# An attention and two-MLP kernel on one core: where block means of V are read from, when weights are decoded, and in which order sums are taken

## The chip, the cores and the metric

One Trainium2 chip, one core. The metric is the device time of one execution, in microseconds. A core has five engines with instruction streams of their own: PE (TensorE, matrix products), DVE (VectorE), ACT (ScalarE), POOL (GpSimd) and SP (SyncE, which here only issues DMAs). Each works through its stream in order and waits on semaphores.

## What is computed

Block-sparse attention feeds two MLPs. The reference, cut to what matters:

```
k_sum = k.reshape(B, H, nb, 32, D).max(axis=3)
v_sum = v.reshape(B, H, nb, 32, D).mean(axis=3)
scores_l = scale * q @ k.T           # kept where |i - j| < 16
scores_s = scale * q @ k_sum.T + log(32)
a = softmax(concat(scores_l, scores_s))
x = a @ concat(v, v_sum)             # B, H, S, D = 2, 8, 768, 64
x = x.reshape(1536, 512)
h = x @ w_in;  x = (h - tanh(h)) @ w_out      # 512 -> 2048 -> 512
a = x @ w1;  b = x @ w2                       # 512 -> 1024
out = ((a * b) @ w3) @ w_out2                 # 1024 -> 1024 -> 512
```

All of it is float32. The large products are taken as three products of fp32r parts (high x high, high x low, low x high), with `split_mm` (L185).

## The kernel before

**Weights.** `Weights` (L60) turns each 128x512 weight chunk, which arrives as 64-bit words, into an fp32 tile and then into a high and a low part. One chunk is a unit: `start` loads it and lets ACT make its size (L108); `unit`, or three times `dve`, lets DVE make the three bit operations L111, L113 and L115; `high` is a cast on ACT (L143), `low` a subtraction on POOL (L150). `need` forces all of it for a chunk that a product is about to read. At most four raw chunks are in SBUF (`NRAW`), so a load on SP waits until DVE is through with an older chunk.

**Attention** (L264 to L490). The 8 pairs of (batch, two heads) are n; each has three groups u of four 64-query tiles, so g = 3n + u runs from 0 to 23, and the loop runs on to 27 to drain. In step g the engines are given: scores of g + 1 (L339), transposes of g - 2 (L367), values of g - 3 (L382), softmax of g (L350 on DVE, L353 on ACT, L360 on POOL). A tile sees a window of 96 keys and 24 blocks. `vg` holds, for every tile, the values of its 96 window keys and, in rows 64 to 87, the 24 block means. These means come from a second copy of V in its natural layout, `vn` (`load_v`, L281): `value_blocks` (L312) multiplies each 128-row piece by a matrix `mean` of 1/32 (6 products per n, each recorded as two), `value_copy` (L322) takes the result from PSUM, and `block_rows` (L326) spreads it into `vg` by three small DMAs. `key_blocks` (L291) makes the block maxima of K, whose last step is a POOL copy into `kt` (L308). `parts` (the table `N34`) spreads the product w3 x w_out2, `w34a`, over the steps; from g = 15 two parts run in each. `busy(8)` (L399) multiplies the identity by itself eight times into an unused bank: before the first scores, and after steps 0 and 1.

**First MLP** (L614 to L635). A step n does one 128-wide column of `w_in` for 512 tokens: `hidden(n)` (L513, tile `ph`), then the curve h - tanh(h) of it (`curve`, L521), and `back(n - 2)` (L545, tile `x`), which multiplies the curve's high and low parts `gh`, `gl` by `w_out`. In each step the loop places `wt.start`, `wt.high`, `evacuate`, `curve` (in which `wt.unit` stands between the end of the curve before and the curve itself), and `wt.low`.

**Second MLP** (L742 to L818). For tokens 512 to 1535 the products with w1 and w2 are taken by a seven-product scheme: `group` (L715) makes seven accumulations `p_w` in four PSUM banks, in the order 1, 6, 5, 7, 2, 4, 3, and combines them on DVE (L668) into four tiles. `w_sums` (L689) prepares the summed weights `s_w` of the next group: two additions of 128x512 (`t0`, `t1`), then four of 128x256. `between` (L776) puts an output product, `final` (L646), between products 5 and 7.

Of the kernel before, what the change touches and what calls it, by code (L numbers as in the profile page):

```python
# [7 lines left out]
F32 = mybir.dt.float32  # L8
# [33 lines left out]
LAG = 2  # L42
NDEC = 3
# [12 lines left out]
def fused_kernel(tc, qT, kT, vN, vW, w_in, w_out, w1, w2, w3, wo2, out):  # L56
# [138 lines left out]
    with tc.tile_pool(name="base", bufs=1) as base, \  # L195
# [19 lines left out]
        mean = base.tile([P, P // BLK + BLK], F32, name="mean")  # L215
        nc.gpsimd.memset(mean, 0.0)
        for i in range(P // BLK):
            nc.gpsimd.memset(mean[i * BLK:(i + 1) * BLK, P // BLK + i:P // BLK + i + 1], 1.0 / BLK)
# [45 lines left out]
        with tc.tile_pool(name="p1", bufs=1) as p1, \  # L264
                tc.tile_pool(name="ps1", bufs=1, space=PSUM) as ps1:
            NG = B * NP * NU
            kt, qt, vn, vg, vrow, st, nm, pr, z = ({} for _ in range(9))
# [13 lines left out]
            def load_v(n):  # L281
                vn[n] = p1.tile([P, S // P, P], F32, tag="vn", bufs=2, name=f"vn_{n}")
                nc.sync.dma_start(out=vn[n], in_=vN[n // NP, n % NP])

            def load_vwin(n):
                vg[n] = p1.tile([P, NQ, P], F32, tag="vg", bufs=2, name=f"vg_{n}")
                nc.sync.dma_start(out=vg[n], in_=vW[n // NP, n % NP])
# [24 lines left out]
            def value_blocks(n, out):  # L312

                pvs[n] = out
                nj = S // P // NBR
                for j in range(nj):
                    for c in range(NBR):
                        o = P // BLK * (1 - j)
                        mm(out=out[c * BLK:(c + 1) * BLK, :], lhsT=mean[:, o:o + BLK], rhs=vn[n][:, c * nj + j, :],
                           start=j == 0, stop=j == nj - 1)  # L320
# [84 lines left out]
            busy(8)  # L405
            load_k(0)
            load_q(0)
            load_v(0)
            wt.load(1)
            load_k(1)  # L410
            load_q(1)
            wt.load(2)
            load_vwin(0)
# [5 lines left out]
            for g in range(NG + 4):  # L419
# [4 lines left out]
                if u == 0 and 0 < n < NN:  # L424
                    load_vwin(n)
                if u == (0 if n else 2) and n + 2 < NN:
                    load_k(n + 2)
                if u == (0 if n else 1) and n + 1 < NN:
                    load_v(n + 1)
# [25 lines left out]
                if g < 2:  # L455
                    busy(8)
# [3 lines left out]
                for i in range(TU):  # L460
# [6 lines left out]
                    if i:  # L467
# [5 lines left out]
                wt.start(2 if g in MORE else 1)  # L473
# [47 lines left out]
        def curve(n, ph, prev):  # L521

            if prev is not None:
                mask, t, g = prev
                nc.vector.copy_predicated(out=g, mask=mask[:, :].bitcast(U32), data=t)  # L525
            wt.unit()
# [6 lines left out]
            if prev is not None:  # L533
                gp[n - 1] = tmp("gh", n, LAG + 1, F32R), tmp("gl", n, LAG + 1, F32R)
                nc.scalar.copy(out=gp[n - 1][0], in_=g)  # L535
                low_part(nc.gpsimd, gp[n - 1][1], g, gp[n - 1][0][:, :])
# [332 lines left out]
```

## Time and profile before

| what | value |
|---|---|
| median of 3 runs | 592.7 us (590.75 to 592.89) |
| profiled execution | 592.24 us, its span 590.4 us |
| PE, share of span and instructions | 97%, 3168 |
| DVE | 79%, 885 |
| ACT | 57%, 741 |
| POOL | 47%, 233 |
| DMA | 59.70 MB, mean 101 GB/s |
| mean granted TensorE clock | 0.994 |

The time of an execution is the span from its first to its last instruction plus about 1.8 us around it. Busy shares are means over stages; the attention stage ends near 129 us, the first MLP near 425 us. A matmul's recorded duration includes its way through the array, so products that follow each other overlap: distance from start to start tells the rate.

### The profile page before, as it was taken

The numbers are of one execution on the slowest core, as the hardware profiler recorded it, in microseconds if no ns is written. First come the engines' busy times: TensorE is split into PE (matmuls) and PEld (weight loads), VectorE is DVE, ScalarE is ACT, GpSimd is POOL, SyncE is SP. The second block draws the span as 40 slices with busy tenths as digits, with TensorE's granted clock in tenths as the row PEclk, the third lists the DMA queues.
The fourth block names the chain that finished last, engine by engine and source line by source line (L and its number), as shares of the span: only waits on it lengthen the run. The fifth ranks groups of instructions, "written<-read, shape, count | busy, mean of one in ns | idle before, by whom it ended". The sixth has DMA issues, their size and how long they took to land.

```text
span 590.4 us, 9062 instructions
## 1 busy us (share of the span) xinstructions
PE 571.6 (97%) x3168; PEld 461.4 (78%) x3168; DVE 465.4 (79%) x885; ACT 338.6 (57%) x741; POOL 278.9 (47%) x233
## 2 busy tenths in 40 slices
PE   8989999998999999999999999999999999999997
PEld 6667777776888888888888888888887777888885
DVE  3789988789999995779999978999577576878510
ACT  3689977868788774466767667765233322222110
POOL 3456555555556652224645522557735624526120
PEclk9989999998999999999999999999999999999999
DMA  8899996653333230012223102223000100000021
GB/s 323 297 323 306 333 298 226 188 162 111 104 108 108 73 106 1 0 37 73 95 84 101 43 1 64 80 71 108 1 0 1 72 0 1 1 2 0 1 90 53
DMA packets 19678, 59.70 MB, mean 101 GB/s; under 512 B 2096, under 2 KB 4784, under 8 KB 19632
## 3 DMA queue, kind: packets, MB, share of 16 engines
q1 hardware_dynamic: 19632, 59.12, 30.8%
q8 instruction: 25, 0.41, 0.3%
q14 instruction: 21, 0.17, 0.1%
HBM read 54.79 MB, written 3.15 MB: 98 GB/s over the span
## 4 chain that ended last, share of the span: by engine, by line
PE 76%; DVE 14%; issue 6%; POOL 2%; ACT 1%; DMA 1%; DVEq 0%; POOLq 0%; ACTq 0%
PE x L187 6%; PE x L188 6%; PE x L186 6%; PE ph L187 6%; PE ph L188 6%; PE ph L186 6%; PE p_w L186 3%; PE p_w L187 3%; PE p_w L188 3%; PE o L188 3%; PE o L186 3%; PE o L187 3%; PE s L339 2%; PE busy L403 2%; PE w L188 2%
## 5 line engine op out<-in xcount | busy, mean ns | idle before, releaser
L150 POOL TENSOR_TENSOR wl<-dec,wh 128x512 fp32r<-128x512 f32 x72 | 111.5, 1553 | 48.9 <-ACT wh L143 41.6
L191 POOL TENSOR_TENSOR gl<-g,gh 128x512 fp32r<-128x512 f32 x48 | 65.8, 1371 | 140.5 <-ACT gh L535 75.3
L186 PE MATMUL x<-gh,wh 128*128 128x512 f32 x192 | 75.4, 393 | 1.8 <-ACT gh L535 1.8
L187 PE MATMUL x<-gl,wh 128*128 128x512 f32 x192 | 75.5, 393 | 1.0 <-POOL gl L191 1.0
L188 PE MATMUL x<-gh,wl 128*128 128x512 f32 x192 | 75.4, 393 | 0.0
L186 PE MATMUL ph<-xh,wh 128*128 128x512 f32 x192 | 74.8, 390 | 0.0
L187 PE MATMUL ph<-xl,wh 128*128 128x512 f32 x192 | 74.7, 389 | 0.0
L188 PE MATMUL ph<-xh,wl 128*128 128x512 f32 x192 | 74.7, 389 | 0.0
L115 DVE SCALAR_TENSOR_TENSOR dec<-raw,dec 128x512 uint32<-128x512 uint32 x45 | 62.4, 1387 | 1.5
L530 ACT ACTIVATE u<-ph 128x512 f32<-128x512 f32 x48 | 28.8, 600 | 54.8 <-PE ph L188 54.8
L143 ACT CAST wh<-dec 128x512 fp32r<-128x512 f32 x72 | 44.5, 623 | 13.3 <-DVE dec L115 13.2
L540 DVE TENSOR_TENSOR g<-ph,u 128x512 f32<-128x512 f32 x48 | 32.7, 682 | 19.8 <-ACT th L531 19.8
L525 DVE COPY_PREDICATED g<-mk,th 128x512 f32<-128x512 uint32 x48 | 41.7, 870 | 4.0
L186 PEld LDWEIGHTS x<-gh,wh 128*128 128x128 f32 x192 | 36.5, 190 | 10.3 <-ACT gh L535 2.2
L353 ACT ACTIVATE pr<-pr,nm 128x120 f32<-128x120 f32 x96 | 37.0, 390 | 12.1 <-DVE nm L350 11.8
L187 PEld LDWEIGHTS x<-gl,wh 128*128 128x128 f32 x192 | 36.4, 189 | 9.0 <-POOL gl L191 1.3
L188 PEld LDWEIGHTS x<-gh,wl 128*128 128x128 f32 x192 | 36.4, 190 | 7.5
L187 PEld LDWEIGHTS ph<-xl,wh 128*128 128x128 f32 x192 | 36.1, 188 | 7.5
L186 PEld LDWEIGHTS ph<-xh,wh 128*128 128x128 f32 x192 | 36.0, 188 | 7.5
L188 PEld LDWEIGHTS ph<-xh,wl 128*128 128x128 f32 x192 | 36.1, 188 | 7.4
L542 DVE SCALAR_TENSOR_TENSOR g<-sq,g 128x512 f32<-128x512 f32 x48 | 40.3, 839 | 0.7 <-ACT sq L538 0.6
L191 POOL TENSOR_TENSOR s_w<-s_w,s_w 128x512 fp32r<-128x512 f32 x16 | 20.4, 1292 | 38.9 <-ACT s_w L704 36.0
(153 smaller groups left out, 1423.0 us busy)
## 6 DMA issues: line engine op xcount, KB each, us to landing
raw<-w SPq DMA_DIRECT2D x32, 512.0 KB
raw<-w_in SPq DMA_DIRECT2D x16, 512.0 KB
raw<-w_out SPq DMA_DIRECT2D x16, 512.0 KB
vg<-vW SPq DMA_DIRECT2D x8, 768.0 KB
raw<-wo SPq DMA_DIRECT2D x8, 512.0 KB
kt<-kT SPq DMA_DIRECT2D x7, 544.0 KB
vn<-vN SPq DMA_DIRECT2D x8, 384.0 KB
qt<-qT SPq DMA_DIRECT2D x7, 384.0 KB
```

The costliest lines, as they stand in the source:

```text
L115: lambda tu=tu, su=su, lo=lo: stt(out=tu, in0=lo, scalar=29, in1=su, op0=ALU.logical_shift_right, op1=ALU.bitwise_or)])
L143: nc.scalar.copy(out=h, in_=self.t[n])
L150: nc.gpsimd.tensor_tensor(out=l, in0=self.t[self.n_low], in1=h[:, :].bitcast(F32), op=ALU.subtract)
L186: mm(out=acc, lhsT=lh, rhs=rh, start=start, stop=False)
L187: mm(out=acc, lhsT=lh, rhs=rl, start=False, stop=False)
L188: mm(out=acc, lhsT=ll, rhs=rh, start=False, stop=stop)
L191: eng.tensor_tensor(out=out, in0=x, in1=high.bitcast(F32), op=ALU.subtract)
L353: nc.scalar.activation(out=pr[g][:, i, :], in_=pr[g][:, i, :], func=AF.Exp, scale=-1.0, bias=nm[g][:, i:i + 1], accum_out=z[g][:, i:i + 1])
L525: nc.vector.copy_predicated(out=g, mask=mask[:, :].bitcast(U32), data=t)
L530: nc.scalar.activation(out=u, in_=ph, func=AF.Square)
L540: nc.vector.tensor_tensor(out=gn, in0=ph, in1=u, op=ALU.mult)
L542: nc.vector.scalar_tensor_tensor(out=gn, in0=sq, scalar=GAM, in1=gn, op0=ALU.add, op1=ALU.mult)
```

## The change

Three separate edits.

1. **Block means from the window tiles.** The copy `vN` and `load_v` go. `value_blocks` reads `vg` instead: 12 tiles of 64 keys per n in place of 6 pieces of 128, so 12 products in place of 6. `mean` is built differently: of a tile's 128 rows, 16 to 47 are the tile's first block, 48 to 63 and 88 to 103 its second; POOL builds these columns with memsets, six `affine_select` and one addition. `vg` gets three buffers in place of two; it is loaded in step u = 1 of the n before, not in u = 0 of its own. Each `busy(8)` becomes `busy(4)`.
2. **First steps of the first MLP.** In steps 0 to 3 (`FIRST`) the curve comes ahead of `wt.start` and of the weight units, and the casts of the step before come ahead of the curve. Steps 0 and 1 decode no unit; in steps 2 and 3 one is decoded behind the curve. The attention's last step decodes and starts none.
3. **Sums in two parts.** `w_sums` yields after its two 128x512 additions; the four 128x256 additions and the casts follow only after the next piece of `group`.

```diff
-        mean = base.tile([P, P // BLK + BLK], F32, name="mean")
+        mean = base.tile([P, 6 + BLK], F32, name="mean")
         nc.gpsimd.memset(mean, 0.0)
-        for i in range(P // BLK):
-            nc.gpsimd.memset(mean[i * BLK:(i + 1) * BLK, P // BLK + i:P // BLK + i + 1], 1.0 / BLK)
+        def rows(col, a, b):
+            nc.gpsimd.memset(col, 1.0 / BLK)
+            for base_, step in ((-a, 1), (b - 1, -1)):
+                nc.gpsimd.affine_select(out=col, in_=col, pattern=[[0, 1]], compare_op=ALU.is_ge, fill=0.0,
+                                        base=base_, channel_multiplier=step)
+        rest = base.tile([P, 1], F32, name="mean_rest")
+        rows(mean[:, 6:7], WIN, WIN + BLK)
+        rows(mean[:, 7:8], WIN + BLK, QT)
+        rows(rest, CW, CW + WIN)
+        nc.gpsimd.tensor_tensor(out=mean[:, 7:8], in0=mean[:, 7:8], in1=rest, op=ALU.add)
...
-                nj = S // P // NBR
-                for j in range(nj):
+                nt = NQ // NBR
+                for j in range(nt):
                     for c in range(NBR):
-                        o = P // BLK * (1 - j)
-                        mm(out=out[c * BLK:(c + 1) * BLK, :], lhsT=mean[:, o:o + BLK], rhs=vn[n][:, c * nj + j, :],
-                           start=j == 0, stop=j == nj - 1)
+                        o = 6 - 2 * j
+                        mm(out=out[c * BLK:(c + 1) * BLK, :], lhsT=mean[:, o:o + BLK], rhs=vg[n][:, c * nt + j, :],
+                           start=j == 0, stop=j == nt - 1)
...
-            busy(8)
+            busy(4)
             load_k(0)
             load_q(0)
-            load_v(0)
             wt.load(1)
+            load_vwin(0)
...
-                if u == 0 and 0 < n < NN:
-                    load_vwin(n)
-                if u == (0 if n else 1) and n + 1 < NN:
-                    load_v(n + 1)
+                if u == 1 and n + 1 < NN:
+                    load_vwin(n + 1)
...
-                    if i:
+                    if i and g < NG + 3:
                         wt.dve(1)
...
-                wt.start(2 if g in MORE else 1)
+                if g < NG + 3:
+                    wt.start(2 if g in MORE else 1)
...
             if prev is not None:
                 mask, t, g = prev
                 nc.vector.copy_predicated(out=g, mask=mask[:, :].bitcast(U32), data=t)
-            wt.unit()
+                if n < FIRST:
+                    high()
+            if n >= FIRST:
+                wt.unit()
...
+            if n < FIRST:
+                cur = curve(n, nxt, cur)
             wt.start()
...
-            wt.high()
+            if LAG <= n < FIRST:
+                wt.unit()
+            if n >= LAG:
+                wt.high()
             closing = len(evac)
             evacuate()
-            cur = curve(n, nxt, cur)
+            if n >= FIRST:
+                cur = curve(n, nxt, cur)
...
                 tt(t, h[:, :].bitcast(F32), add, l[:, :].bitcast(F32))
+            yield
             a, b = slice(0, H * P), slice(H * P, DM)
...
-            lhs = w_sums("w2", m)
-            for _ in range(4):
+            sums = w_sums("w2", m)
+            next(sums)
+            next(g)
+            lhs = next(sums)
+            for _ in range(3):
                 next(g, None)
```

`high()` in `curve` is the pair of the cast `gh` and the subtraction `gl`. The w2 group of each m takes its sums for the next w1 group in the same two parts. The changed file's lines are numbered up to 24 higher.

PE at the start of the program, before (`s` are scores, `pvs` the means of n = 0, `busy` the identity products):

```order
L403 MATMUL busy<-ident 128x128 x8
L339 MATMUL s_176<-kt_151,qt_154 64x120 x8
L339 MATMUL s_185<-kt_151,qt_154 64x120 x8
L403 MATMUL busy<-ident 128x128 x8
L339 MATMUL s_226<-kt_151,qt_154 64x120 x8
L319 MATMUL pvs<-vn_157,mean 32x128 x6
L403 MATMUL busy<-ident 128x128 x8
L339 MATMUL s_291<-kt_161,qt_163 64x120 x8
```

and in the change:

```order
L411 MATMUL busy<-ident 128x128 x4
L347 MATMUL s_173<-kt_150,qt_153 64x120 x8
L347 MATMUL s_182<-kt_150,qt_153 64x120 x8
L411 MATMUL busy<-ident 128x128 x4
L347 MATMUL s_215<-kt_150,qt_153 64x120 x8
L327 MATMUL pvs<-vg_158,mean 32x128 x12
L411 MATMUL busy<-ident 128x128 x4
L347 MATMUL s_278<-kt_160,qt_162 64x120 x8
```

The rows stand in the same places; the identity products are halved and the means doubled.

DVE where attention passes into the first MLP, before (`xl` closes attention, `dec` are weight units, `g` and `th` the curve):

```order
L191 TENSOR_TENSOR xl_122<-av_1920,xh_119 128x256
L113 SCALAR_TENSOR_TENSOR dec_1943<-raw_1853,dec_1943 128x512
L115 SCALAR_TENSOR_TENSOR dec_1943<-raw_1853,dec_1943 128x512
L111 TENSOR_SCALAR dec_1958<-dec_1958 128x512
L113 SCALAR_TENSOR_TENSOR dec_1958<-raw_1896,dec_1958 128x512
L115 SCALAR_TENSOR_TENSOR dec_1958<-raw_1896,dec_1958 128x512
L540 TENSOR_TENSOR g_2011<-ph_1984,u_2007 128x512
L541 TENSOR_TENSOR th_2009<-ph_1984,th_2009 128x512
L542 SCALAR_TENSOR_TENSOR g_2011<-sq_2008,g_2011 128x512
L525 COPY_PREDICATED g_2011<-mk_2010,th_2009 128x512
L111 TENSOR_SCALAR dec_1997<-dec_1997 128x512
```

and in the change:

```order
L192 TENSOR_TENSOR xl_129<-av_1935,xh_126 128x256
L552 TENSOR_TENSOR g_2009<-ph_1992,u_2005 128x512
L553 TENSOR_TENSOR th_2007<-ph_1992,th_2007 128x512
L554 SCALAR_TENSOR_TENSOR g_2009<-sq_2006,g_2009 128x512
L536 COPY_PREDICATED g_2009<-mk_2008,th_2007 128x512
L552 TENSOR_TENSOR g_2041<-ph_2019,u_2037 128x512
L553 TENSOR_TENSOR th_2039<-ph_2019,th_2039 128x512
L554 SCALAR_TENSOR_TENSOR g_2041<-sq_2038,g_2041 128x512
L536 COPY_PREDICATED g_2041<-mk_2040,th_2039 128x512
L552 TENSOR_TENSOR g_2073<-ph_2051,u_2069 128x512
L553 TENSOR_TENSOR th_2071<-ph_2051,th_2071 128x512
L554 SCALAR_TENSOR_TENSOR g_2073<-sq_2070,g_2073 128x512
```

No weight unit stands between the curves of steps 0, 1 and 2; three units come that much later.

DVE in the first w1 group, before (`t_w` and `s_w` are the sums, the last row reads the bank of product 5 for the last time):

```order
L668 TENSOR_TENSOR t_w_0_4994<-wh_3787,wl_3788 128x512
L668 TENSOR_TENSOR t_w_0_4995<-wh_4161,wl_4162 128x512
L668 TENSOR_TENSOR s_w_0_4996<-t_w_0_4995 128x256
L668 TENSOR_TENSOR s_w_0_4996<-s_w_0_4996,t_w_0_4994 128x256
L668 TENSOR_TENSOR s_w_0_4997<-t_w_0_4994,t_w_0_4995 128x256
L668 TENSOR_TENSOR s_w_0_4997<-t_w_0_4994,s_w_0_4996 128x256
L661 COPY u_out_0_5013<-o_0_4577 128x512
L661 COPY gh_out_2_5025<-o_2_4585 128x512
L668 TENSOR_TENSOR a_1_4967<-a_1_4967,p_w_0_5034 128x512
L668 TENSOR_TENSOR ab_0_4968<-a_1_4967,p_w_0_4986 128x512
```

and in the change:

```order
L686 TENSOR_TENSOR t_w_0_5009<-wh_3802,wl_3803 128x512
L686 TENSOR_TENSOR t_w_0_5010<-wh_4176,wl_4177 128x512
L679 COPY u_out_0_5018<-o_0_4592 128x512
L679 COPY gh_out_2_5030<-o_2_4600 128x512
L686 TENSOR_TENSOR a_1_4982<-a_1_4982,p_w_0_5039 128x512
L686 TENSOR_TENSOR ab_0_4983<-a_1_4982,p_w_0_5001 128x512
L686 TENSOR_TENSOR s_w_0_5011<-t_w_0_5010 128x256
L686 TENSOR_TENSOR s_w_0_5011<-s_w_0_5011,t_w_0_5009 128x256
L686 TENSOR_TENSOR s_w_0_5012<-t_w_0_5009,t_w_0_5010 128x256
L686 TENSOR_TENSOR s_w_0_5012<-t_w_0_5009,s_w_0_5011 128x256
```

The four 128x256 sums stand behind the last row that reads the bank; the same happens in the six other groups that prepare sums.

## Rows read from the trace of the kernel before

**Rows 1.** The page's 40 slices, 14.8 us each: busy tenths of PE and DVE.

```profile
PE   8989999998999999999999999999999999999997
...
DVE  3789988789999995779999978999577576878510
```

**Rows 2.** Waits of PE, whole run: waiting line, releaser; total us, times, longest.

```profile
PE s L339 <- POOL kt L308: 4.9, 6, 1.5
PE p_w L186 <- DVE ab L668: 3.2, 3, 1.4
```

**Rows 3.** Timeline of the first 25 us: start, us, engine, line, operation, tiles; idle before.

```profile
1.36 6.77 PE L403 MATMUL busy<-ident 128*128 128x128 f32 x16 [1.36 <-POOL ident masks.py:199]
...
2.19 0.26 POOL L210 TENSOR_SCALAR_AFFINE_SELECT band<-band 64x96 f32<-64x96 f32 x1
...
3.04 0.47 POOL L218 MEMSET mean<- 32x1 f32 x4
...
5.31 0.42 POOL L308 COPY kt<-kb 128x288 f32<-128x288 f32 x1 [0.22 <-DVE kb L307]
...
8.05 3.24 PE L339 MATMUL s<-kt,qt 64*64 64x120 f32 x32
10.09 0.28 DVE L350 CUSTOM_DVE_ANT_0 pr<-s,mask 128x120 f32<-128x120 f32 x1 [4.84 <-PE s L339]
...
11.23 4.32 PE L403 MATMUL busy<-ident 128*128 128x128 f32 x16
...
16.44 0.64 PE L319 MATMUL pvs<-vn,mean 128*32 128x128 f32 x12
...
16.56 0.28 DVE L350 CUSTOM_DVE_ANT_0 pr<-s,mask 128x120 f32<-128x120 f32 x1 [0.47 <-PE s L339]
...
23.02 0.28 DVE L350 CUSTOM_DVE_ANT_0 pr<-s,mask 128x120 f32<-128x120 f32 x1 [3.50 <-PE t L367]
```

**Rows 4.** Windows of 10 us: busy us of each engine, clock, DMA share, GB/s.

```profile
50.00:60.00 10.00, 9.17 (x127) 7.25 (x122) 9.49 (x41) 9.13 (x31) 5.78 (x6) 1.00 0.99 337
```

**Rows 5.** Timeline of PE late in attention, block means of n = 5.

```profile
75.48 0.64 PE L319 MATMUL av<-vn,mean 128*32 128x128 f32 x12
```

**Rows 6.** Timeline of attention's end and the first steps of the first MLP.

```profile
125.50 0.69 DVE L115 SCALAR_TENSOR_TENSOR dec<-raw,dec 128x512 uint32<-128x512 uint32 x1
...
131.62 0.39 PE L186 MATMUL ph<-xh,wh 128*128 128x512 f32 x1
...
133.45 0.59 ACT L530 ACTIVATE u<-ph 128x512 f32<-128x512 f32 x1
133.62 1.48 POOL L150 TENSOR_TENSOR wl<-dec,wh 128x512 fp32r<-128x512 f32 x1 [1.28 <-ACT wh L143]
...
133.99 1.67 DVE L115 SCALAR_TENSOR_TENSOR dec<-raw,dec 128x512 uint32<-128x512 uint32 x1
...
135.03 0.72 ACT L539 ACTIVATE mk<-u,numax 128x512 f32<-128x512 f32 x1
...
137.56 0.73 DVE L525 COPY_PREDICATED g<-mk,th 128x512 f32<-128x512 uint32 x1
...
138.99 0.49 PE L186 MATMUL x<-gh,wh 128*128 128x512 f32 x1 [1.77 <-ACT gh L535]
...
140.50 0.69 PE L187 MATMUL x<-gl,wh 128*128 128x512 f32 x1 [1.02 <-POOL gl L191]
```

**Rows 7.** Windows of 2 us at the first back products; columns as in rows 4.

```profile
142.00:144.00 2.00, 2.00 (x7) 1.52 (x6) 1.86 (x5) 0.96 (x3) 0.14 (x1) 0.50 0.70 242
144.00:146.00 2.00, 2.00 (x10) 1.67 (x9) 1.97 (x2) 2.00 (x4) 1.62 (x2) 0.99 0.05 20
```

**Rows 8.** Timeline of DVE in groups w1 and w2.

```profile
466.44 0.42 DVE L668 TENSOR_TENSOR s_w<-t_w 128x256 f32<-128x256 f32 x1
...
469.89 0.69 DVE L668 TENSOR_TENSOR ab<-a,p_w 128x512 f32<-128x512 f32 x1
...
505.41 0.69 DVE L668 TENSOR_TENSOR b<-b,p_w 128x512 f32<-128x512 f32 x1 [0.53 <-PE p_w L188]
```

More of the change, by code (lines that the diff above doesn't have):

```diff
@@ L42 @@
 LAG = 2
+FIRST = 4
 NDEC = 3
@@ L53, with fused_kernel @@
 SS, SB, GAM = 0.23012508654699032, 0.2896718893925817, 0.2494235093653836
-def fused_kernel(tc, qT, kT, vN, vW, w_in, w_out, w1, w2, w3, wo2, out):
+def fused_kernel(tc, qT, kT, vW, w_in, w_out, w1, w2, w3, wo2, out):
     nc = tc.nc
@@ L266, in fused_kernel @@
             NG = B * NP * NU
-            kt, qt, vn, vg, vrow, st, nm, pr, z = ({} for _ in range(9))
+            kt, qt, vg, vrow, st, nm, pr, z = ({} for _ in range(8))
             def load_k(n):
@@ L279, in load_q @@
                     nc.sync.dma_start(out=qt[n][:, i[0]:i[1]], in_=qT[n // NP, n % NP, :, i[0]:i[1]])
-            def load_v(n):
-                vn[n] = p1.tile([P, S // P, P], F32, tag="vn", bufs=2, name=f"vn_{n}")
-                nc.sync.dma_start(out=vn[n], in_=vN[n // NP, n % NP])
             def load_vwin(n):
-                vg[n] = p1.tile([P, NQ, P], F32, tag="vg", bufs=2, name=f"vg_{n}")
+                vg[n] = p1.tile([P, NQ, P], F32, tag="vg", bufs=3, name=f"vg_{n}")
                 nc.sync.dma_start(out=vg[n], in_=vW[n // NP, n % NP])
@@ L412, in fused_kernel @@
             wt.load(2)
-            load_vwin(0)
             for i in range(3):
@@ L455, in fused_kernel @@
                 if g < 2:
-                    busy(8)
+                    busy(4)
                 wt.high()
@@ L521, in curve, with high @@
         def curve(n, ph, prev):
+            def high():
+                gp[n - 1] = tmp("gh", n, LAG + 1, F32R), tmp("gl", n, LAG + 1, F32R)
+                nc.scalar.copy(out=gp[n - 1][0], in_=g)
+                low_part(nc.gpsimd, gp[n - 1][1], g, gp[n - 1][0][:, :])
             if prev is not None:
@@ L532, in curve @@
                 cur = mask, t, gn
[L533 to L536, printed above, removed]
+            if prev is not None and n >= FIRST:
+                high()
             if ph is not None:
@@ L706, in w_sums @@
                 lhs[i[0]], lhs[i[1]] = (h, l, 0), (h, l, H * P)
-            return lhs
+            yield lhs
         def seventh(acc, lhs, i):
@@ L749, in fused_kernel @@
                 wt.free += [(rawp, "raw", "raw", NRAW)] * NRAW
-                lhs = w_sums("w1", 0)
+                _, lhs = w_sums("w1", 0)
             a = product_a(m, 0)
@@ L800, in fused_kernel @@
             next(g)
-            if m + 2 < NM:
-                lhs = w_sums("w1", m + 2)
+            more = m + 2 < NM
+            if more:
+                sums = w_sums("w1", m + 2)
+                next(sums)
             for a, b in ((a22, b22), (a11, b11), (a21, b21)):
                 next(g)
+                if more and a is a22:
+                    lhs = next(sums)
                 tt(a, a, ALU.mult, b)
@@ L846 @@
     vw[:, :, np.r_[0:QT, CW:NC]] = vp[:, rows].reshape(B, WK, NQ, NP, P).transpose(0, 3, 1, 2, 4)
-    vn = vp[:, WIN:WIN + S].reshape(B, S // P, P, NP, P).transpose(0, 3, 2, 1, 4)
     w3 = moe2_w3.T.reshape(NM // 2, 2, P, NM // 2, 2 * P).transpose(3, 0, 2, 1, 4)
@@ L851 @@
         "kT": kt,
-        "vN": np.ascontiguousarray(vn),
         "vW": vw,
```

## The prediction

> **What bounds the kernel now.** I read the page's slices first, then the waits of PE, then the timeline wherever PE waits. PE is busy in nine tenths of nearly every slice [rows 1], so time is won only where PE stands idle or works slowly. The longest waits are on the block maxima copied by POOL, 4.9 us in six, and on DVE in the second MLP, 3.2 us in three [rows 2]; the start of the first MLP has two more, 1.77 and 1.02 us [rows 6]. In attention the busy share misleads: in the ten microseconds from 50 on, DVE is busy 9.49 and ACT 9.13 of 10 [rows 4], and PE's waits there are the shadow of theirs. So from the first softmaxes until about 75 us DVE sets the pace, and an earlier start of DVE is kept. From 75 us on two weight parts run per step and PE sets it.
>
> All sums start from the profiled execution, 592.24 us, which is 0.46 below the median of the three runs.
>
> **Start of attention.** The first scores wait behind sixteen recorded identity products, 6.77 us from 1.36, although their last input, POOL's copy into `kt`, ends at 5.31 + 0.42 = 5.73 [rows 3]. Halved, the block ends at 4.8 and the copy decides. But POOL has more to do ahead of it: four memsets (0.47 us) become three, with six selects and an addition. If a select costs what a memset does (0.12) that is 0.7 us more, if what the 64x96 select does, started every 0.32 us, 2.1; I take 1.4, near the middle, since the selects wait for each other but are narrow. POOL was free 0.2 us before the copy, so the scores start near 7.0, not 8.05: 1.05 us won.
>
> DVE then has the work from 10.09 to 16.56 less its wait of 0.47, 6.0 us [rows 3], and starts its third softmax near 15.0 (before 16.56). The third one ends 2.96 us later (16.56 to 23.02 less 3.50), at 18.0. The next one waits for the transpose that frees its buffer, which stands on PE behind two more identity blocks of 4.32 us, each halved to 2.16, and behind the means, whose twelve recorded products, about 0.6 us from 16.44, become twenty-four. PE: scores until 10.3, block 12.45, scores 13.4, means 14.6, block 16.75, scores and transpose 1.65 as before (23.02 less the end of the block there, 16.44 + 0.6 + 4.32), 18.4. DVE resumes at about 18.2, not at 23.02: **-4.8**. ACT and POOL had waited with it. Their next loads are covered: SP issues the window tile (768 KB) in the slot after the first weight chunk, 2.2 MB into the queue, done near 8 us at the 337 GB/s of rows 4, and is needed at 13.4. The bounds: POOL's cheaper end gives -5.9; the other end comes from the clock.
>
> An identity pair takes 6.77 / 8 = 0.85 us in the first block and 4.32 / 8 = 0.54 in the second [rows 3]: the array ran at its lower level of 1.2 GHz through all of the first block and reached 2.4 GHz only about when the 32 dense score products ended. So by these rows the identity products do not raise the clock, and fewer of them cost nothing. If without them the clock stayed low until the fourth scores, the blocks would be 3.4 each, the means 2.3, scores and transpose 1.4 more: DVE resumes near 23.3, **+0.3**.
> The Trainium skill (TensorE: Matmul & The Clock Gate, Part 1, "What's actually happening") speaks against the cut: the slow clock is the default and activity is what releases it. By that rule the term would be the +0.3, by the row it is -4.8.
>
> **Means of the later pairs.** Six more products for each of n = 1 to 7, about 0.6 us more on PE each. For n = 1 to 4 DVE sets the pace and PE's wait for the `kt` copy, on average 0.8 us once per pair [rows 2], takes it in. For n = 5, 6, 7 (75.48 [rows 5] and two more like it) PE sets the pace: 3 x 0.6 = 1.8, of which the short waits left there hide a little. **+1.5**; between +0.4 (hidden by the waits) and +2.8 (n = 4 and another exposed as well). What hides the first ones are waits that vanish if DVE gets faster. The removed loads, 8 x 384 KB of 59.7 MB, relieve a queue that is 0.99 busy [rows 4], but no engine waits for a weight chunk there, so I give them nothing of their own.
>
> **Start of the first MLP.** PE ends the third `ph` at 138.99 - 1.77 = 137.2, then waits for `gh` and `gl` of step 0 until 140.50, and its clock falls to the lower level: granted 0.50 in 142 to 144, where 7 products start against 10 in the next two microseconds [rows 6, 7]. Start to start is 0.43 us in place of 0.23 for eight of twelve products, 1.7 us. So 1.77 + 1.02 + 1.7 = 4.5 lost. Step 0's curve is late since ACT's `u` stands at 133.45 behind the cast of a unit, and DVE's part behind the last operation of the next (133.99, 1.67 us), although PE was done with the first `ph` when the second began, at 131.62 [rows 6]. In the change nothing stands between: `u` at 131.8; until `mk` 2.3 us as from 133.45 to 135.75; the predicated copy 0.73; the cast 0.62; POOL's part 1.5 as from the first to the second `x` product: 137.0, and PE needs it at 137.4. No wait remains.
> What pays: three units come three steps later. They are needed from step 12 on, one is decoded per step, and DVE has room near 221 to 266 us (5, 7, 7 tenths [rows 1]). In steps 2 and 3, however, the unit now stands ahead of the predicated copy, so `gl` of steps 2 and 3 comes later. Worked through the order with units of 1.8 us (three operations of up to 0.69), the second of them is 0.3 us late for PE. **-4.2**, between -1.5 (rival 2) and -4.5, all of it.
> That 1.8 rests on POOL being idle then: L115 takes 0.69 us at 125.50 with no POOL instruction beside it, and 1.67 at 133.99, inside POOL's subtraction of 133.62 to 135.10 [rows 6]. With POOL beside both units they end 2 us later, and `gl` of step 3 misses PE by 1.8 in place of 0.3.
> The Trainium skill (SBUF — State Buffer, "Who interferes with whom") has a rule for such pairs: a DVE instruction with two SBUF inputs and a POOL instruction that reads SBUF block each other for the whole instruction. The trace agrees with that, 1.67 against 0.69. By that rule, should POOL run beside them, the term is that of the second rival below, -1.5.
>
> **Groups.** The four half-width sums take 1.65 us of DVE (four of 0.42 from 466.44, 0.41 apart) and stand ahead of the additions that free the bank of product 5, ending with 469.89 [rows 8]. PE waits there in three groups, 3.2 us in all and 1.4 at most [rows 2]; with a restart each, which I put at 0.1, 3.5. Moved behind, the additions end 1.65 earlier, which ends all three waits. But the sums now stand ahead of the addition that frees the bank of the next group's second product, and of the casts and POOL subtractions that feed it; working through, 0.3 comes back after the second, 0.3 after the third, and 0.2 in the later groups, where DVE had waited 0.53 for product 7 [rows 8] and now has the sums behind it. **-2.7**, between -1.0 and -3.5.
>
> **Sum.** -4.8 + 1.5 - 4.2 - 2.7 = -10.2: 592.24 - 10.2 = **582.0 us**. All best ends together give 578.7, all worst 592.8.
>
> **Rivals.**
> 1. *The early start is given back.* The clock stays low, or the loads (0.99 busy in rows 4) cannot be moved forward by 5 us. For: a queue without room; against: a tenth of attention's bytes is gone, and SP waits for free buffers, not for bytes. First term +0.3 in place of -4.8: 587.
> 2. *The wait moves on.* POOL runs beside the units of steps 2 and 3; PE then waits 1.8 us in two pieces at the fourth `x`, and the clock may fall as at 142 [rows 7], another 1.7. The term is -1.5: 585. For: POOL's subtractions follow every step; against: between them it is idle here.
> 3. *Slower: the window tile arrives late.* The means now need 768 KB, issued two steps ahead, about 8.6 us (28 steps in the 121 us from 8 to 129), where 384 KB had been issued three ahead. If issue to landing takes over 8.6 us in a queue 0.99 busy, PE waits in order and everything behind it. At 12 us that is 3.4 us for each of seven pairs, +24 against gains of 10: 606; it turns to a loss from about 10 us per transfer. Against: 768 KB take 2.3 us at 337 GB/s, and about a weight chunk or two stand ahead.
> 4. *Nothing comes of it in attention or the groups*, since DVE's work is the same and only its order differs; half of the transition alone: 590.
>
> **Chances.** Forecast 0.56, rival 1 0.17, rival 2 0.13, rival 4 0.08, rival 3 0.06. A change under 0.5%, 3 us, cannot be told from none here. Forecast and rivals 1 and 2, and a little of 4, lie beyond that: faster 0.87; the rest of 4 is the same, 0.08; rival 3 is slower, 0.05 as it may only eat the gains. The range: from 578, just under the best ends, to 588, which takes in rivals 1 and 2 and leaves out 3 and 4.
>
> **What would show it.** Right: DVE's fourth softmax at 18 to 19 us, first scores near 7; the means' rows twice as many at 0.57 us per twelve; no wait on `gh` or `gl` at the first `x` and clock 1.00 there; no wait of `p_w` on `ab` above 0.4. Wrong: identity pairs at 0.85 beyond 12 us; PE waiting for DMA at the means; a wait on `gl` two steps later; `p_w` waiting for POOL's `s_w`.

## The result, and the profile after

The change takes **584.72 us** (median of four, 583.37 to 587.65) where the kernel before takes 592.73: a ratio of 0.987 with a 95% interval of 0.984 to 0.990, so 8.0 us or 1.3% faster. The forecast was 582.0, the range 578 to 588. The profiled execution of the change took 583.37 us (span 581.7), the fastest of its four; that of before had 592.24 (590.4). So the two traces show 8.7 us, somewhat more than the medians.

Three points of the program split the spans without a gap: the first `ph` product (attention ends on PE), the start of the seventh back product `x`, from which on the steps are 5.44 us apart in both, and the end.

| stretch | before | after | difference | forecast |
|---|---|---|---|---|
| start to first `ph` | 128.77 | 125.63 | -3.1 | -4.8 + 1.5 = -3.3 |
| first `ph` to seventh `x` | 45.87 | 43.67 | -2.2 | -4.2 |
| seventh `x` to the end | 415.76 | 412.4 | -3.4 | -2.7 |

Busy tenths of PE and DVE in the page's 40 slices after, which answer to [rows 1]: the first two slices of PE fall by one each, and DVE is fuller in the first three.

```profile
PE   7889999999999999999999999999999999999997
...
DVE  4999897766999999679999978999668587778610
```

The waits of PE in the whole run of the change (waiting line, releaser; total us, times, longest), which answer to [rows 2]:

```profile
PE s L347 <- POOL kt L316: 5.7, 7, 2.2
PE av L390 <- DMA vg<-vr: 3.1, 3, 1.6
PE x L188 <- POOL gl L192: 1.6, 2, 1.3
PE busy L411 <- POOL ident masks.py:199: 1.4, 1, 1.4
PE w L189 <- POOL wl L151: 0.2, 1, 0.2
```

The wait of `p_w` on `ab` is gone whole. A new one has come: the value products `av` wait for `vg<-vr`, the three small DMAs that spread the block means. Of the 5.7 on `kt`, 2.2 are the start, now that the identity products end before the copy.

The window from 50 to 60 us and the means of the sixth pair after, which answer to [rows 4] and [rows 5]: DVE is as busy as before, the DMA share 0.90 for 0.99, and twice the products take 1.07 us for 0.64.

```profile
50.00:60.00 10.00, 8.66 (x124) 7.00 (x123) 9.49 (x43) 9.57 (x34) 5.67 (x7) 1.00 0.90 288
```

```profile
71.08 1.07 PE L327 MATMUL av<-vg,mean 128*32 128x128 f32 x24
```

The start of the program, timeline after, which answers to [rows 3]:

```profile
1.43 3.36 PE L411 MATMUL busy<-ident 128*128 128x128 f32 x8 [1.43 <-POOL ident masks.py:199]
...
3.29 0.44 POOL L223 TENSOR_SCALAR_AFFINE_SELECT mean<-mean 128x1 f32<-128x1 f32 x2
...
6.48 0.42 POOL L316 COPY kt<-kb 128x288 f32<-128x288 f32 x1
...
6.96 3.47 PE L347 MATMUL s<-kt,qt 64*64 64x120 f32 x32 [2.17 <-POOL kt L316]
...
10.35 2.17 PE L411 MATMUL busy<-ident 128*128 128x128 f32 x8
...
13.42 1.07 PE L327 MATMUL pvs<-vg,mean 128*32 128x128 f32 x24
...
18.25 0.28 DVE L358 CUSTOM_DVE_ANT_0 pr<-s,mask 128x120 f32<-128x120 f32 x1 [0.36 <-PE t L375]
...
21.30 0.69 PE L390 MATMUL av<-pt,vg 120*64 120x64 f32 x16 [1.64 <-DMA vg<-vr]
```

Scores at 6.96 and DVE's fourth softmax at 18.25, 4.77 earlier than before: the forecast said 7.0 and 18.2. POOL's selects take 0.22 us each, and its copy starts 1.17 later than before, as worked (1.4 of new work, less the 0.2 that POOL had been idle). Then the last row takes 1.64 us back.

Attention's end and the first steps of the first MLP, timeline after, which answers to [rows 6]:

```profile
128.68 0.60 ACT L544 ACTIVATE u<-ph 128x512 f32<-128x512 f32 x1 [1.26 <-PE ph L189]
...
131.79 0.75 DVE L536 COPY_PREDICATED g<-mk,th 128x512 f32<-128x512 uint32 x1
...
132.58 0.62 ACT L531 CAST gh<-g 128x512 fp32r<-128x512 f32 x1 [1.03 <-DVE g L536]
...
133.92 0.39 PE L187 MATMUL x<-gh,wh 128*128 128x512 f32 x1
...
134.62 0.50 PE L188 MATMUL x<-gl,wh 128*128 128x512 f32 x1 [0.31 <-POOL gl L192]
...
147.79 0.69 DVE L116 SCALAR_TENSOR_TENSOR dec<-raw,dec 128x512 uint32<-128x512 uint32 x1
...
148.40 0.75 DVE L536 COPY_PREDICATED g<-mk,th 128x512 f32<-128x512 uint32 x1
148.51 0.62 ACT L144 CAST wh<-dec 128x512 fp32r<-128x512 f32 x1 [2.04 <-DVE dec L116]
...
149.05 0.68 ACT L109 ACTIVATE dec<-raw 128x512 f32<-128x512 f32 x1
...
149.49 1.67 DVE L114 SCALAR_TENSOR_TENSOR dec<-raw,dec 128x512 uint32<-128x512 uint32 x1
...
149.63 0.58 ACT L544 ACTIVATE u<-ph 128x512 f32<-128x512 f32 x1
...
150.10 0.58 ACT L545 ACTIVATE th<-ph 128x512 f32<-128x512 f32 x1
...
150.58 0.61 ACT L531 CAST gh<-g 128x512 fp32r<-128x512 f32 x1
...
151.33 1.69 POOL L192 TENSOR_TENSOR gl<-g,gh 128x512 fp32r<-128x512 f32 x1 [0.72 <-PE ph L189]
...
153.07 0.50 PE L188 MATMUL x<-gl,wh 128*128 128x512 f32 x1 [1.32 <-POOL gl L192]
```

The first back product waits 0.31 us in all, where it had waited 1.77 and 1.02. The fourth one, which had waited for nothing, now waits 1.32 for its `gl`. The clock no longer falls, neither at the first back product nor at the fourth; windows of 2 us after, columns as in [rows 7]:

```profile
134.00:136.00 2.00, 1.69 (x8) 1.16 (x7) 1.78 (x3) 1.96 (x4) 0.57 (x1) 1.00 0.00 0
136.00:138.00 2.00, 2.00 (x11) 1.65 (x10) 0.86 (x2) 1.00 (x2) 0.30 (x1) 1.00 0.00 0
...
154.00:156.00 2.00, 2.00 (x11) 1.64 (x10) 1.93 (x4) 1.42 (x3) 0.66 (x1) 1.00 0.43 176
```

DVE in the first w1 group, timeline after, which answers to [rows 8]: the addition that frees the bank stands ahead of the sums, and behind the sums DVE waits 1.68 us for PE.

```profile
463.02 0.69 DVE L686 TENSOR_TENSOR ab<-a,p_w 128x512 f32<-128x512 f32 x1
463.62 0.42 DVE L686 TENSOR_TENSOR s_w<-t_w 128x256 f32<-128x256 f32 x1
...
468.65 0.69 DVE L686 TENSOR_TENSOR b<-u_b,p_w 128x512 f32<-128x512 f32 x1 [1.68 <-PE p_w L189]
```

### The profile page after: what moved, and what is told of

Same layout as the page of the kernel before. It is cut to its first block, busy times and chain, and to the rows that moved or that the text cites. A ratio compares the mean times of both kernels' runs of the same rounds, so it can differ in the third digit from the quotient of the medians.

```text
span 581.7 us, 9203 instructions
## 1 busy us (share of the span) xinstructions
PE 565.4 (97%) x3240; PEld 458.3 (79%) x3240; DVE 462.1 (79%) x885; ACT 339.1 (58%) x741; POOL 280.8 (48%) x239
## 4 chain that ended last, share of the span: by engine, by line
PE 73%; DVE 12%; issue 5%; ACT 3%; DMA 3%; POOL 2%; SPq 0%; POOLq 0%; DVEq 0%; ACTq 0%
PE x L188 6%; PE x L187 6%; PE x L189 6%; PE ph L187 6%; PE ph L188 6%; PE ph L189 6%; PE p_w L187 4%; PE p_w L189 4%; PE p_w L188 4%; PE o L187 3%; PE o L189 3%; PE o L188 3%; PE w L189 2%; PE w L188 2%; PE w L187 2%
## 5 line engine op out<-in xcount | busy, mean ns | idle before, releaser
L116 DVE SCALAR_TENSOR_TENSOR dec<-raw,dec 128x512 uint32<-128x512 uint32 x45 | 60.7, 1348 | 1.5
L192 POOL TENSOR_TENSOR s_w<-s_w,s_w 128x512 fp32r<-128x512 f32 x16 | 22.9, 1449 | 43.5 <-ACT s_w L723 23.5
L536 DVE COPY_PREDICATED g<-mk,th 128x512 f32<-128x512 uint32 x48 | 39.7, 826 | 4.2 <-DVE g L554 0.5
```

Source lines behind the costliest of these rows:

```text
L116: lambda tu=tu, su=su, lo=lo: stt(out=tu, in0=lo, scalar=29, in1=su, op0=ALU.logical_shift_right, op1=ALU.bitwise_or)])
L192: eng.tensor_tensor(out=out, in0=x, in1=high.bitcast(F32), op=ALU.subtract)
```

## The experiments

Twelve kernels in three sets of four, each set timed beside the kernel before; the ratio is to that one. The table splits each profiled execution as above; a profile is one execution, the median stands for all. The column to the first `ph` scatters most: four profiles whose attention code is the change's (the change, no unit in step 3, early cast, unit moved) lie between 125.4 and 129.6, three with that of before (before, first steps alone, sums alone) between 128.8 and 131.2. A difference of two or three microseconds in this column alone shows nothing.

| kernel | median us | ratio to before, interval | to first `ph` | to seventh `x` | to the end |
|---|---|---|---|---|---|
| before | 592.3 to 592.9 | | 128.77 | 45.87 | 415.8 |
| the change | 584.72 | 0.987, 0.984 to 0.990 | 125.63 | 43.67 | 412.4 |
| means alone | 594.26 | 1.003, 1.002 to 1.005 | 129.55 | 47.05 | 416.2 |
| four identity products alone | 589.82 | 0.996, 0.994 to 0.997 | 126.76 | 45.91 | 415.7 |
| first steps alone | 590.02 | 0.997, 0.994 to 1.000 | 131.17 | 43.67 | 415.7 |
| sums alone | 588.9 | 0.995, 0.993 to 0.996 | 128.98 | 45.88 | 412.1 |
| change, no identity products | 583.47 | 0.983, 0.979 to 0.987 | 126.55 | 43.66 | 412.2 |
| change, rows ahead of loads | 588.84 | 0.992, 0.989 to 0.995 | 131.33 | 43.65 | 412.3 |
| change, no unit in step 3 | 591.36 | 0.997, 0.994 to 1.001 | 125.42 | 49.10 | 412.3 |
| change, early cast in step 4 | 585.61 | 0.987, 0.983 to 0.992 | 129.57 | 44.14 | 412.3 |
| change, copy of V loaded again | 589.08 | 0.993, 0.991 to 0.996 | 132.14 | 43.66 | 412.3 |
| four identity products, one copy of V | 588.01 | 0.992, 0.990 to 0.995 | 123.22 | 45.79 | 415.8 |
| change, unit moved to step 4 | 584.77 | 0.987, 0.985 to 0.990 | 127.46 | 43.43 | 412.8 |
| the same, no identity products | 583.63 | 0.985, 0.984 to 0.987 | 125.66 | 43.38 | 412.9 |

**Means alone.** The kernel before with edit 1, `busy(8)` kept:

```diff
-            busy(4)
+            busy(8)
```

(shown against the change; edits 2 and 3 are undone as well).

> The kernel before with edit 1 alone, the identity products left at eight. Theory (the extra products cost PE time in the late pairs, nothing else changes): scores still start near 8.05 us, DVE's fourth softmax moves from 23.0 to about 23.5 because 12 more mean products stand ahead of it, and n = 5 to 7 add 3 x 0.45 = 1.35: 592.2 + 1.9 = 594.1 us. Rival (the waits of the value products for the spread mean rows, 2.7 us in the changed kernel, come from the larger and earlier window transfers and not from the early start): the same waits show here, about 596.8 us.

Measured 594.26, as the theory had it, but not where. In the profile attention is only 0.8 us longer; another 1.2 stand in the transition, where the clock stayed low longer (0.66 over 140 to 150 us, 0.83 before). One wait for the rows is there, 1.1 us. So in this profile's attention the extra products do not show their whole 1.9 us. Its clock has 1.00 from 30 to 35 us, where the profile of before has 0.66: the absent fall pays for part of them, by chance or through the missing copy of V.

**Four identity products alone.** `busy(8)` becomes `busy(4)` in the kernel before.

> The kernel before with the identity products halved and nothing else. Theory (the identity products only delay, and what the start wins is partly given back by the mean rows that arrive through a full queue): scores near 5.9 us, identity pairs at 0.85 us in the first block and 0.54 in the second, DVE's fourth softmax at 17.4 (won 5.6), then 1.5 to 2.7 us of waits for the mean rows: the kernel gains 3 to 4.5, 588 to 589 us. Rival 1 (the queue has room): no such waits, 586.5. Rival 2 (the identity products are what raises the clock): pairs of 0.85 beyond 12 us and no gain, 592.

Measured 589.82, 2.5 us won of the 5.8 that the start alone gives (the fourth softmax at 17.26 for 23.02). PE waits 3.2 us for the rows, and the clock falls. PE's timeline, then windows of 2 us as in [rows 4]:

```profile
21.27 1.12 PE L382 MATMUL av<-pt,vg 120*64 120x64 f32 x16 [1.33 <-DMA vg<-vr]
```

```profile
18.00:20.00 2.00, 0.62 (x4) 0.41 (x4) 1.35 (x5) 1.97 (x6) 0.24 (x1) 0.97 0.81 136
20.00:22.00 2.00, 0.73 (x14) 0.73 (x16) 2.00 (x7) 1.20 (x7) 1.99 (x2) 0.50 0.83 260
22.00:24.00 2.00, 2.00 (x28) 1.46 (x26) 0.83 (x7) 0.93 (x2) 0.00 (x0) 0.50 0.89 278
```

The scores start 1.4 us earlier than in the change, yet the value products start at 21.27, in the change at 21.30. PE is busy 1.35 of the 4 us from 18 to 22 and drops to 1.2 GHz. SP can issue the rows only at 15.76 here: they write into the window tile, whose load has to land first, and SP waits 3.0 us for it (releaser; total us, times, longest):

```profile
SPq L329 <- DMA vg<-vW: 3.0, 1, 3.0
```

The two halves of edit 1, measured alone, give 1.9 - 2.5 = -0.6 us; in the change edit 1 gains more, 2.3 by the medians (8.0 less the 2.3 and 3.4 of the next two runs), 3.1 in the profile.

**First steps alone.** Edit 2 in the kernel before.

> The kernel before with edit 2 alone. Theory (the first two waits and the fall of the clock, 4.5 us, go, and a new wait of 1.3 us for the low part at the fourth back product and some tenths elsewhere stay, whatever attention did before): -2.2, 590.0 us. Rival (the wait at the fourth back product came from the earlier end of attention, not from the order of the first steps): no such wait here and -4.2, 588.0 us.

Measured 590.02, with an interval that just reaches no change; the trace decides. The second stretch is 43.67, to the hundredth that of the change, with the same wait of 1.3 at the fourth back product, which thus belongs to the order of the first steps. (Attention was 2.4 us longer in this execution than in before's, with the same code up to its last step: the clock fell twice in it.)

**Sums alone.** Edit 3 in the kernel before.

> The kernel before with edit 3 alone. Theory (the three waits of the group products on the bank of product 5 go and nothing comes in their place): -3.4, 588.8 us, no wait of a group product above 0.2. Rival (some of it comes back through the later summed weights, as predicted): -2.7 with waits of 0.2 to 0.3 in several groups, 589.5 us.

Measured 588.9; the last stretch is 412.1 for 415.8, and no wait of `p_w` is in the list. Nothing comes back.

**No identity products at all.**

```diff
-            busy(4)
             load_k(0)
...
-                if g < 2:
-                    busy(4)
```

> The changed kernel without any identity product (they feed no output). Theory (the dense score products raise the clock by themselves, and the mean rows, which land near 21.3 us whatever PE does, are a wall): the scores start at 6.96 and take 3.5 us as in the change, the third scores then start one every 0.06 us at 2.4 GHz; DVE's fourth softmax starts near 17, but the first value products still start at 21.3; PE stands idle some 2 us longer before them, the clock falls there as it did at 20 us in the run with four identity products alone, and the time is 585 to 587 us. Rival 1 (without identity products the clock stays at 1.2 GHz beyond the first scores): third scores at 0.1 us each and DVE's fourth softmax at 19 or later, 587 to 589. Rival 2 (no wall): value products near 19, 582.5 to 583.5 us.

Measured 583.47, 1.2 below the change, with overlapping intervals: less than the theory feared. PE in the first 16 us:

```profile
6.88 4.12 PE L347 MATMUL s<-kt,qt 64*64 64x120 f32 x48 [6.88 <-POOL kt L316]
11.24 1.08 PE L327 MATMUL pvs<-vg,mean 128*32 128x128 f32 x24 [0.24 <-DMA vg<-vW]
15.45 1.04 PE L347 MATMUL s<-kt,qt 64*64 64x120 f32 x16 [3.13 <-POOL kt L316]
```

In the change 32 such products take 3.4 us, so the last sixteen take well under a microsecond here, where sixteen take 1.87 at 1.2 GHz (below): the scores alone brought the clock to 2.4 GHz at about 10 us. It fell after the idle 3.13 (0.66 over 15 to 20 us), and the value products started at 22.15, yet attention ended only 0.9 us later than in the profile of the change.

**Rows ahead of the loads.**

```diff
                     block_rows(0)
+                    load_k(2)
+                    load_q(2)
```

(both taken out of their earlier places).

> The changed kernel with the loads of the third pair's keys and queries (928 KB) issued behind the first pair's mean rows instead of ahead of them. Theory (the rows wait in the queue for the bytes issued before them): 928 KB at the 400 GB/s of that stretch are 2.3 us, so the rows land near 19 us instead of 21.3, the wait of 1.64 us at the first value products goes, and attention ends 0.5 to 1.6 us earlier: 583.0 to 584.2 us. Rival (what they wait for is their own small packets, or loads issued after them): the wait stays above 1 us, 584.7.

A miss: 588.84, 4 us slower than the change. The rows did come earlier, at 20.55 for 21.30, and their wait fell from 1.64 to 0.61. But SP now issues the moved loads at 17.56 and 18.29, between the rows and the next weight chunk, and this chunk, issued at 19.04 for 17.23, is late in their place. ACT waits 4.7 us for it, where it waits 1.4 in the change, and PE behind ACT:

```profile
ACT bits L109 <- DMA raw<-wo: 4.7, 1, 4.7
```

```profile
PE t L375 <- ACT pt L380: 2.6, 1, 2.6
```

To reorder the loads in that stretch only changed who waited, here at a loss.

**No unit in step 3 of the first MLP.**

```diff
-            if LAG <= n < FIRST:
+            if n == LAG:
                 wt.unit()
```

> The changed kernel without the weight unit in step 3 of the first MLP; all later units come one step later. Theory (that unit, 1.9 us of DVE, is what makes the curve of step 3 late, and with it the fourth back product): its predicated copy starts near 146.7 instead of 148.4, no wait for the low part at the fourth back product, -1.3 to -1.7, 583.2 us. Rival (the unit that is missing is then needed before it is ready near step 12): the wait goes but PE waits for a weight part later, 584.7 or more.

The rival, and worse: 591.36. The waits of PE:

```profile
PE x L189 <- POOL wl L151: 5.1, 1, 5.1
PE x L188 <- POOL gl L192: 0.3, 1, 0.3
```

The `gl` wait at the fourth back product goes, but the product that waits now, 5.1 us for its weight's low part, is that same fourth one: the unit of step 3 is the chunk that it multiplies by.

**Early cast in step 4.**

```diff
-                if n < FIRST:
+                if n <= FIRST:
                     high()
...
-            if prev is not None and n >= FIRST:
+            if prev is not None and n > FIRST:
                 high()
```

> The changed kernel with the cast and the subtraction of step 3's curve placed ahead of the two ACT operations of step 4, as in the steps before. Theory (the late part is ACT's order at step 4: two operations of 0.58 us stand between the predicated copy's end and the cast): the cast starts near 149.7 instead of 150.58, POOL's subtraction near 150.6 behind its weight part, and the wait of 1.32 us falls to 0.4 to 0.7: -0.6 to -0.9, 584.0 us. Rival (it is DVE's unit in step 3 alone): the wait stays above 1 us.

The wait falls to 0.90, less than expected, and a new one of 0.86 on ACT's copy of a finished `x` appears at the next back product; the stretch is 0.5 longer. No gain in the median. The profile shows something else, in attention, whose code is that of the change:

```profile
10.28 3.35 PE L411 MATMUL busy<-ident 128*128 128x128 f32 x8
13.56 1.87 PE L347 MATMUL s<-kt,qt 64*64 64x120 f32 x16
15.36 1.93 PE L327 MATMUL pvs<-vg,mean 128*32 128x128 f32 x24
17.22 2.74 PE L411 MATMUL busy<-ident 128*128 128x128 f32 x8
```

```profile
21.66 0.28 DVE L358 CUSTOM_DVE_ANT_0 pr<-s,mask 128x120 f32<-128x120 f32 x1 [3.22 <-PE t L375]
```

Identity pairs are 0.84 us apart and the means 0.08 until past 18 us: the array stayed at 1.2 GHz through the dense scores and beyond, although the granted clock is recorded as 1.00 from the start, and the fourth softmax started at 21.66 in place of 18.25.

**The removed copy of V loaded again,** into a buffer that nothing reads, and its counterpart, **four identity products with one copy of V**:

```diff
+                    load_v(n + 1)
```

```diff
-rhs=vn[n][:, c * nj + j, :]
+rhs=vn[0][:, c * nj + j, :]
...
-                if u == (0 if n else 1) and n + 1 < NN:
-                    load_v(n + 1)
```

> The changed kernel with the removed copy of V loaded again (384 KB per pair, which no instruction reads); everything else stays. Theory (until about 60 us attention is short of bytes, so the removed 3.1 MB are what lets the early start last): the mean rows land later than 21.3 us, the waits of PE and ACT for transfers grow and the clock falls again in attention; attention ends 1.5 to 3 us later, 586.2 to 587.7 us. Rival (no engine waits for these bytes, as the prediction has it): 584.7 us, waits as in the change.

> The kernel before with four identity products and the natural copy of V loaded for the first pair only: the block means of the other seven pairs are taken from the first pair's V, so their values are left out. Products as in the kernel before, bytes as in the changed one. Theory (bytes decide): against the run with four identity products alone (589.8) the mean rows land earlier, the clock falls less and 2 to 3 us are won: 587 to 588 us, about the changed kernel's attention less its extra products. Rival (it is the twelve extra products per pair, which shorten PE's idle times, that keep the clock up in the changed kernel): 589 to 590, with the clock falling at 20 us as without them.

Both point to the bytes. Loads that nobody reads cost the change 4.4 us (589.08), and the intervals of the two ratios do not meet; the same bytes left out of the kernel with four identity products win 1.8 (588.01 for 589.82, with intervals that just overlap), without one product more. In the first, the rows of the second pair need 9.4 us from the issue of the first of them to the product that they release, in the change 7.4, and PE waits 3.13 us. In the second, the window tile lands sooner, SP waits 1.4 us for it instead of 3.0 and issues the rows at 13.72 instead of 15.76, and the value products start at 19.39 in place of 21.27, with no fall of the clock up to 130 us:

```profile
37.44 1.13 PE L394 MATMUL av<-pt,vg 120*64 120x64 f32 x16 [3.13 <-DMA vg<-vr]
```

```profile
19.39 0.69 PE L382 MATMUL av<-pt,vg 120*64 120x64 f32 x16 [1.13 <-DMA vg<-vr]
```

```profile
SPq L329 <- DMA vg<-vW: 1.4, 1, 1.4
```

The 4.4 us are not the price of the bytes alone, though. The copy was loaded into one buffer, where the kernel before has two, so SP stood still until the first copy had landed, and with it the loads behind:

```profile
SPq L299 <- DMA vn<-vN: 4.1, 1, 4.1
```

How much of the 4.4 this order took is not shown. The profile of this run had its clock at the lower level until about 16 us.

**The unit of step 3 moved into step 4,** behind the predicated copy and the cast; and the same without identity products:

```diff
             if n >= FIRST:
                 wt.unit()
+            if n == FIRST:
+                wt.high()
+                wt.low()
```

(with the edits of the early cast and of the kernel without the unit in step 3).

> The changed kernel with the unit of step 3 decoded in step 4, behind the predicated copy and the cast of step 3's curve, and cast and subtracted at once. Theory (that unit is the weight chunk of the fourth back product itself; it may stand behind the curve of step 3, whose low part then comes near 149.4 us, and its own low part near 151.4): no wait above 0.4 us at the fourth back product, -1.0 to -1.3, 583.5 us. Rival (DVE, POOL and ACT are full there and the wait only changes its name, as it did when the unit was left out or the cast was moved): a wait of 1 us or more for the weight's low part or for the next steps' curves, 584.7 or more.

> The same, and without any identity product. Theory (the two act in different stages and add): 1.2 us below the run with the moved unit alone, 582.2 us. Rival (the waits for the mean rows decide the end of attention, and without identity products PE only idles longer): no difference to the run with the moved unit alone.

584.77 and 583.63. The 1.32 at the fourth back product becomes 0.62 for the weight's low part, and 0.4 for ACT's copy and longer steps behind make up the rest. The second is 1.1 us below the first, as the change without identity products (583.47) is 1.2 below the change; in both pairs the intervals overlap. So no version was found that is measurably faster than the change without identity products, and that one is ahead of the change by less than the intervals tell apart.

## Why the prediction was right, and where it was not

**The sign, the range and two of three stretches** came out as worked: 584.72 lies within 578 to 588. The profile of the change is 1.4 us above 582.0: +2.0 from the transition, -0.7 from the groups, +0.2 from attention. The median lies another 1.3 above that profile, the fastest of the four executions. The two longest of the four, 587.65 and 585.6, have a mean granted clock of 0.997, the other two, near 583.5, have 0.999. What can lie behind 0.997 is seen in the profile with the unit moved (585.37, 0.997, the same attention code): PE waits 2.1 us for the rows of the second pair, the clock has 0.66 from 35 to 40 us, and attention ends 1.8 later than in the profile of the change.

**Start of attention, -4.8:** to the tenth as far as it was worked (18.25). That it is kept did not hold as put. The sentence "no engine waits for a weight chunk there, so I give them nothing of their own" is the step that failed, along with "their next loads are covered", which looked at the window tile and not at the three small row transfers behind it. They are issued from 14.84 us on and let PE go at 21.30; nor was the first sentence true any more, for ACT waits 1.4 us for a weight chunk there. Against that, the fall of the clock that the kernel before has at 31 to 35 us (0.83 over 30 to 40 us) is absent (1.00). Lead of the change at the mean products of the eight pairs: 3.0, 3.1, 3.8, 5.0, 5.0, 4.4, 4.0, 3.6, then 3.1 at the first `ph`. So the 4.8 was down to 3.1 at the second pair, came back to 5.0 at the fourth, and was spent on means from the fifth on. The forecast of -3.3 for attention was met because two things that it left out cancel in this profile: the wait for the rows and the absent fall of the clock. That it was met to 0.2 is luck, as the scatter of this column shows. That the early start lasts is put down to the bytes by the two runs with them put back and left out; how much of it they pay is open. Rival 1 was right that the queue is full and wrong that everything is given back.

The Trainium skill (DMA: Bandwidth & Descriptors, "Queues, rings and completion order") says that each DMA engine takes the descriptors of a queue in ring order. The trace agrees: with the third pair's loads issued ahead, the rows need 6.5 us from the first issue to the products (14.84 to 21.30), with these behind 5.4 (15.20 to 20.55).

**The clock at the start.** The reading that the clock does not rise in the identity products, and rises in the dense scores, held in the two kernels without identity products (2.4 GHz at about 10 and 12 us). It does not hold every time: in two of the six profiles with the change's start (the early cast, and the copy loaded again) the low level lasted to almost 19 and to 16 us. In the four profiles with eight identity products that was not seen, but four are too few to rule it out. That is the prediction's other end (+0.3), as a matter of chance from one execution to the next; the early cast's profile paid 3.4 us for it. The recorded clock of that profile is 1.000, so the low level at the start does not show in it; the two longer executions of the change, at 0.997, must have had a fall that does, and whether their clock rose late as well no profile shows.
The Trainium skill (TensorE: Matmul & The Clock Gate, Part 1, "What's actually happening") says that the number of slow products at the start of one kernel varies between runs. The profiles agree: the rise stood at 10.4 us in one and almost at 19 in another of the same attention code.

**Means of later pairs, +1.5:** from the fifth pair on the lead falls by 0.4 to 0.6 a pair, 1.8 in all. The sum was right within 0.3, its parts less so: four exposed pairs (n = 4 as well) at some 0.45 in place of three at 0.6.

**Start of the first MLP, -4.2: wrong by half.** The first wait and the fall of the clock went, as worked; of the second wait 0.31 us stayed, since the predicated copy starts 3.1 us after `u` (128.68 to 131.79) and not 2.3: three DVE operations stand between. The step that failed is "the second of them is 0.3 us late for PE". The units did take 1.8 us with POOL idle (L116 at 0.69 beside no POOL instruction), so rival 2's cause did not come in; but its place did. The working had the predicated copy's cast follow at once, as in steps 0 to 3. Step 4 keeps the old order, and there ACT has two operations on weights and two of the next curve ahead of the cast: from the copy's end at 149.15 to 150.58. Then POOL takes 1.69, beside DVE, where it takes 1.29 alone. The third and fourth back steps take 5.84 and 7.17 us in place of 5.44, 2.1 too much where 0.3 had been worked. ACT's order is only a part of this: the early cast took 0.4 off the wait and brought 0.86 elsewhere, and no run won more than 0.3 us of the stretch back, so which engine limits there stays open. And "needed from step 12 on" was false: the unit of step 3 is the fourth back product's own weight, which is why it could be neither left out nor moved with profit.
The Trainium skill (SBUF — State Buffer, "Who interferes with whom") names such pairs of DVE and POOL; the trace agrees in both directions, DVE's L114 at 1.67 beside POOL's `wl`, and POOL's `gl` at 1.69 beside DVE's L116.

**Groups, -2.7:** the waits went, the 0.8 us that was to come back did not: -3.4 in the change, -3.6 alone. In the first w1 group DVE waits 1.68 us for PE behind the sums, so they fit in there.

**Rival 3** was far off: the window tile is never waited for in the change. **Rival 4** fell with the first two rows of the table.

**Sums that do not come out.** None of these changes the forecast. POOL's cheaper end, 0.7 us less, gives -5.5 for the start and not -5.9. The -1.5 of rival 2 lies between the wait alone (-2.7) and the wait with the fall (-1.0). The operation of 1.67 us begins inside POOL's subtraction but ends 0.56 behind it. The four sums take 1.47 us from start to start and not 1.65, which still covers the longest wait of 1.4.

## What to carry to other kernels

Where the DMA share is near 1, as in this attention, a transfer that no engine visibly waits for can still have a price: ask which small transfer stands behind it in the queue, and which issue on SP waits for it. Two edits measured alone need not add up; here one removed the bytes that stood in the way of the other's early start. A stretch of one profile can be off by more than the effect that is looked for: count on medians, or on several profiles of the same code. Before moving a producer later, look up which consumer it feeds, and follow its path through every engine into the first step that keeps the old order.

## What the runs showed of the hardware

The time at which the clock rises at the start of one and the same attention code lay between 10.4 and almost 19 us, and the recorded clock has 1.00 all the while. In the run with four identity products PE stood idle 1.48 us before 19.32 and again 1.33 us before 21.27, and the clock fell to 1.2 GHz at about 20 us; after the single wait of 1.64 us in the change it did not fall. The length of a fall varied too: after the same two waits at the first back product, 1.8 and 1.0 us, the window from 140 to 150 us had 0.83 in one kernel and 0.66 in another.
